# Parameter rows on GpSimd's DMA queue, a first FFN1 pass between the x transposes, a row copy on GpSimd, and a last store in three parts

## The chip, the cores and the metric

The kernel runs on one core of one Trainium2 chip. The metric is the device time of one execution in microseconds (us). The profile's span is about 1.7 us shorter than that time, because it starts and ends a little inside it. TensorE (PE), VectorE (DVE), ScalarE (ACT), GpSimd (POOL) and SyncE (SP) each have their own list of instructions in this program. DMAs are issued here from SP, ACT and, in the changed kernel, GpSimd.

## The reference

It is a gated mix of a state-space layer and a feed-forward layer, with S = 2048, D = 448, F = 1792, in bf16.

```python
g = sigmoid((x * gate_w).sum(-1, keepdims=True))
dt = exp(log_dt);  Lam = Lambda_re + 1j * Lambda_im
Lam_bar = exp(dt * Lam)
B_bar = ((Lam_bar - 1) / Lam)[:, None] * (B_re + 1j * B_im)
h[t] = Lam_bar * h[t-1] + x[t] @ B_bar.T                  # 2048 steps
a = 2 * (h @ (C_re + 1j * C_im).T).real + x * Dskip
b = silu(x @ w1) @ w2
out = g * a + (1 - g) * b
```

## The kernel before

The kernel handles even and odd rows of x apart. Each thunk goes into the list of one engine, and a tracker adds the semaphore waits. The parts that matter lie in the first 17 us. The loads of the head, in order of issue on their queues:

```python
ld_w("sp", 0)                                     # W1 rows 0..127, first 768 columns, 192 KB
for i, (eng, v) in enumerate((("sp", A_log_dt), ("sp", A_Lambda_re),
                              ("act", A_Lambda_im), ("act", A_Dskip))):
    ld(eng, R[i:i + 1, 0:D], row(v), ...)         # four rows of 0.9 KB
ld_w("act", 1)                                    # W1 rows 128..255, 192 KB
ld_w("sp", 2)
ld("act", W1E[0:64, 3, :], B_w1[384:448, :], "W1Ea")      # W1's last 64 rows ...
ld("act", W1E[64:128, 3, :], B_w1[384:448, :], "W1Ez")    # ... and a second copy
ld("sp", W1E[:, 0:3, FA:], ..., "W1Ed")           # all other columns, 768 KB
# then BB (two of 336 KB) on ACT, transposes of x on SP, and LT (transposes of BB) later
```

TensorE begins with seven matmuls on zeros, to warm up, then 16 transposes of x, then the first FFN1 pass. This pass fills six PSUM banks, with one block of W1 rows (j) after the other:

```python
warm(NWARM)
...                                # 16 transposes of x into banks 4..7, copied to XT by VectorE
def ffn1_first():
    for j in range(4):
        for fb, bank in enumerate(banks):          # banks 0..5
            pe.matmul(ps[:, bank, :], W1E[p, j, fb*128:(fb+1)*128], XT[p, j, 0:512], ...)
            if j == 1 and fb == 2: yield           # here: the parameter transpose, mm_cols
```

`mm_cols` turns the four parameter rows R into columns. VectorE copies them to PV, ACT makes exponentials and sines of them, and only after these does ACT evacuate banks 0 to 5 (silu into AT). The main FFN1 stream (the "whole" matmuls of three row blocks and the "half-row" matmuls of W1's last 64 rows, two at a time, from the two copies) takes banks in turn: 6 and 7, then 0 and 1 again. The last of the eight output tiles is stored in two parts:

```python
parts = ((slice(0, D), ["_00"]), (slice(D, 2 * D), ["_10", "_11"])) if kt == NKT - 1 else ...
```

## Time and profile before

| kernel before | us |
|---|---|
| time, median of 3 runs | 153.32 (152.78 to 153.47) |
| span of the profiled run | 152.1 |
| TensorE takes up W1's first row block | 6.24 |
| parameter transpose | 8.53 |
| main FFN1 stream starts | 13.91 |
| last VectorE instruction ends; to the span's end | 149.89; 2.2 |

The lines of the page, the chain, TensorE and the SP queue are shown in the prediction. Two more matter for what follows. First the ACT queue in the timeline (start in us from the span's start, duration of the issues, queue, what):

```profile
1.74 0.54 ACTq L208 DMA_DIRECT2D R<-in_A_Lambda_im_dram  x1
2.31 0.24 ACTq L208 DMA_DIRECT2D R<-in_A_Dskip_dram  x1
2.58 1.59 ACTq L208 DMA_DIRECT2D W1E<-in_B_w_dram  x3
```

The two small rows go first. ACT's block of W1 is issued at 2.58, which is 0.85 us after SP issued the first block (1.73). Second, the matmuls of the first pass in the view of the tile W1E (count, ns minimum/median/maximum, first and last start in us, forms):

```profile
L330 PE MATMUL ps<-XT,W1E x24: 376/379/390, 6.2 to 11.8; 128*128 128x512 bf16 x18, 64*128 64x512 bf16 x6
```

All 24 have nearly the same duration. The 0.379 us is that of one matmul from end to end; they follow each other at 0.216 us. This is the fast pace. The seven matmuls on zeros, from 1.26 us on, followed each other at about 0.427; the fast pace began among the x transposes, at 4.4 us.

### The profile page before, as it was taken

How to read it: one execution, taken by the hardware profiler on the slowest of the kernel's cores; microseconds unless marked ns; L12 is line 12 of the kernel's file. 1: busy time of each engine (PE TensorE's matmuls, PEld its weight loads, DVE VectorE, ACT ScalarE, POOL GpSimd, SP SyncE). 2: the span in 40 equal slices, each digit the busy share in tenths (PEclk: the TensorE clock that was granted, in tenths of full speed). 3: DMA queues.
4: the chain of work that ended last, by engine and by line, in shares of the span. 5: the costliest groups of instructions: out<-in, count | busy, mean ns of one | idle time of the engine just before them, and what ended most of it. 6: DMA issues, size and time to landing. Idle time of an engine off the chain costs nothing.

```text
span 152.1 us, 2020 instructions
## 1 busy us (share of the span) xinstructions
PE 146.1 (96%) x756; PEld 69.2 (46%) x756; DVE 121.1 (80%) x234; ACT 64.1 (42%) x111; POOL 5.4 (4%) x15
## 2 busy tenths in 40 slices
PE   6797999999999999999999999999999999999993
PEld 2432434344444455433555443555555555555552
DVE  1648989999999999999999999999980017876333
ACT  0358559999978513174731294513133110000000
POOL 7000220000000000000000000000000000000000
DMA  4999999989999100485280000000000001111221
GB/s 150 240 259 233 267 287 157 224 169 168 288 318 321 49 0 0 90 151 104 51 245 6 0 0 4 2 0 0 0 0 4 0 0 60 60 60 60 92 94 60
DMA packets 26401, 16.25 MB, mean 107 GB/s; under 512 B 17940, under 2 KB 25112, under 8 KB 26392
## 3 DMA queue, kind: packets, MB, share of 16 engines
q1 hardware_dynamic: 23668, 12.46, 33.7%
q10 hardware_dynamic: 2724, 3.67, 9.6%
q8 instruction: 6, 0.10, 0.3%
q14 instruction: 3, 0.02, 0.1%
HBM read 9.93 MB, written 1.84 MB: 77 GB/s over the span
## 4 chain that ended last, share of the span: by engine, by line
PE 89%; DMA 7%; SPq 1%; DVE 0%; issue 0%
PE ps L634 28%; PE ps L298 22%; PE ps L750 14%; PE ps L650 14%; DMA W1E<-in_B_w_dram 7%; PE ps L754 4%; PE ps L313 4%; PE ps L665 4%; SPq L208 1%; SPq L237 1%; DVE OT L761 0%; PE ps L667 0%
## 5 line engine op out<-in xcount | busy, mean ns | idle before, releaser
L634 PE MATMUL ps<-W,AT 128*128 128x448 bf16 x224 | 43.0, 352 | 0.0
L340 ACT ACTIVATE AT<-ps 128x512 bf16<-128x512 f32 x56 | 29.2, 620 | 13.0 <-PE ps L313 12.5
L634 PEld LDWEIGHTS ps<-W,AT 128*128 128x128 bf16 x224 | 21.8, 98 | 20.6 <-issue 0.2
L639 ACT ACTIVATE LT<-ps,GT 128x448 bf16<-128x448 f32 x16 | 10.1, 634 | 31.3 <-PE ps L634 27.6
L650 PE MATMUL ps<-XT,LT 128*128 128x512 bf16 x98 | 21.3, 379 | 0.0
L298 PE MATMUL ps<-XT,W1O 128*128 128x512 bf16 x84 | 19.1, 379 | 0.0
L761 DVE SCALAR_TENSOR_TENSOR OT<-ps,GT,LT 128x448 bf16<-128x448 f32 x8 | 5.5, 684 | 14.8 <-PE ps L754 14.7
L686 DVE TENSOR_TENSOR_SCAN G<-P,Q 128x1024 f32<-128x1024 f32 x7 | 15.7, 2278 | 0.0
L298 PE MATMUL ps<-XT,W1E 128*128 128x512 bf16 x66 | 14.9, 380 | 0.1
L650 PEld LDWEIGHTS ps<-XT,LT 128*128 128x128 bf16 x98 | 9.6, 98 | 11.5
L298 PEld LDWEIGHTS ps<-XT,W1O 128*128 128x128 bf16 x84 | 7.9, 98 | 10.6 <-issue 1.7
L750 PE MATMUL ps<-CO,HS 128*128 128x448 bf16 (+1 forms) x63 | 11.9, 332 | 0.0
L750 PE MATMUL ps<-CE,HS 128*128 128x448 bf16 x56 | 11.9, 352 | 0.0
L298 PEld LDWEIGHTS ps<-XT,W1E 128*128 128x128 bf16 x66 | 6.1, 98 | 8.7 <-issue 1.3
L654 ACT ACTIVATE HS<-ps 128x512 bf16<-128x512 f32 x14 | 8.5, 633 | 3.2 <-PE ps L650 2.7
L761 DVE SCALAR_TENSOR_TENSOR OT<-ps,GT,W1E 128x448 bf16<-128x448 f32 (+1 forms) x9 | 5.7, 632 | 4.7 <-PE ps L750 4.7
L601 DVE SCALAR_TENSOR_TENSOR JK<-W1O,GWB 128x448 bf16<-128x448 bf16 x16 | 8.8, 618 | 0.0
L683 DVE TENSOR_TENSOR Q<-G,SIN 128x1024 bf16<-128x1024 f32 x7 | 8.5, 1219 | 0.0
L683 DVE TENSOR_TENSOR Q<-G,COS 128x1024 bf16<-128x1024 f32 x7 | 8.5, 1209 | 0.0
L750 PEld LDWEIGHTS ps<-CO,HS 128*128 128x128 bf16 x63 | 6.1, 98 | 4.7
L750 PEld LDWEIGHTS ps<-CE,HS 128*128 128x128 bf16 x56 | 5.5, 98 | 5.1
L754 PE MATMUL ps<-KT,XT 128*128 128x448 bf16 x32 | 7.4, 352 | 0.0
(84 smaller groups left out, 145.3 us busy)
## 6 DMA issues: line engine op xcount, KB each, us to landing
W1O<-in_A_x_dram ACTq DMA_DIRECT2D x1, 1792.0 KB, 14.4
W<-in_B_w_dram SPq DMA_DIRECT2D x1, 1568.0 KB, 8.1
out_dram<-OT SPq DMA_DIRECT2D x7, 224.0 KB, 2.0
W1O<-in_B_w_dram SPq DMA_DIRECT2D x1, 1344.0 KB, 8.7
W1E<-in_A_x_dram SPq DMA_DIRECT2D x1, 896.0 KB, 6.1
W1E<-in_B_w_dram SPq DMA_DIRECT2D x1, 768.0 KB, 10.6
W1E<-in_B_w_dram ACTq DMA_DIRECT2D x2, 224.0 KB, 8.1
W1O<-in_B_w_dram SPq DMA_DIRECT2D x2, 224.0 KB, 5.0
```

What stands on the lines that cost most here:

```text
L298: ins = pe.matmul(ps[:, bank, :], W[:, w0 + j, fb * 128:(fb + 1) * 128], XT[:, x0 + j, hs], start=(j == 0 and not rest_first), stop=(j == ...
L340: T.op("act", lambda e: e.activation(a[:, fb, :], ps[:, bank, :], AF.Silu), reads=[f"ps{bank}"], writes=[f"AT{c % 2}_{fb}"])
L601: T.op("dve", lambda e, t=t: e.scalar_tensor_tensor(JK[:, t % 2, :], XN[:, t * D:(t + 1) * D], 1.0, GWB[:, :], ALU.mult, ALU.mult, accum_o ...
L634: ins = pe.matmul(ps[:, bank, 0:D], a[:, fb, q * 128:(q + 1) * 128], W2[:, fb, :], start=(fb == 0), stop=(fb == NFB - 1))
L639: T.op("act", lambda e: e.activation(bs(tile), ps[:, bank, 0:D], AF.Copy, scale=GT[:, 2, tile:tile + 1]), reads=[f"ps{bank}", "GT2"], writ ...
L650: ins = pe.matmul(ps[:, bank, :], LT[:, m, j, :], XT[:, j, h * 512:(h + 1) * 512], start=(j == 0), stop=(j == 6))
L654: T.op("act", lambda e: e.activation(HS[:, m, 8 + h * 512:8 + (h + 1) * 512], ps[:, bank, :], AF.Copy), reads=[f"ps{bank}", f"F{pt}"], wri ...
L683: T.op("dve", lambda e: e.tensor_tensor(o, a, b, op), reads=reads, writes=writes)
L686: T.op("dve", lambda e: e.tensor_tensor_scan(G[:, c, :], rb, Q1[:, c, :], 0.0, ALU.mult, ALU.add), reads=[f"Q1{c}", "rr"], writes=[f"G{c}"])
L750: ins = pe.matmul(ps[:, b, c], HS[:, m, o0:o0 + 128], C[:, m, c], start=(m == 0), stop=(odd == 1 and m == 6))
L754: ins = pe.matmul(ps[:, b, c], XT[:, j, t0:t0 + 128], KT[:, j, c], start=False, stop=(j == 3))
L761: T.op("dve", lambda e, b=b, c=c: e.scalar_tensor_tensor(o[:, odd * D:(odd + 1) * D][:, c], ps[:, b, c], GT[:, 1, tile:tile + 1], (BG[:, k ...
```

## The change

The four parts aim at the head and the tail. (1) The parameter rows go on GpSimd's queue, so that SP and ACT are free for W1 sooner. (2) TensorE transposes only half of the x tiles, runs the j = 0 part of the first pass, and transposes the rest. (3) The second copy of W1's last 64 rows is no longer loaded but copied by GpSimd. (4) The last store is in three parts.

```diff
         ld_w("sp", 0)
-        for i, (eng, v) in enumerate((("sp", A_log_dt), ("sp", A_Lambda_re), ("act", A_Lambda_im), ("act", A_Dskip))):
-            ld(eng, R[i:i + 1, 0:D], row(v), f"R{i}", gR if i < 2 else gR2)
         ld_w("act", 1)
         ld_w("sp", 2)
         ld("act", W1E[0:64, 3, :], B_w1[384:448, :], "W1Ea")
-        ld("act", W1E[64:128, 3, :], B_w1[384:448, :], "W1Ez")
 ...
+        for i, v in enumerate((A_log_dt, A_Lambda_re, A_Lambda_im, A_Dskip)):
+            ld("pool", R[i:i + 1, 0:D], row(v), f"R{i}", gR)
 ...
+        for i, c in enumerate((slice(FA, FA + 512), slice(FA + 512, F_FF), slice(0, FA))):
+            T.op("pool", lambda e, c=c: e.tensor_copy(W1E[64:128, 3, c], W1E[0:64, 3, c]), reads=["W1Ea"],
+                 writes=[f"W1Ez{i}"])
 ...
-                    if j == 1 and fb == 2:
+                    if (j, fb) in ((0, NFA - 1), (1, 2)):
                         yield
 ...
+        xpose(0)
+        xpose(1)
         first = ffn1_first()
         next(first)
-        T.op("pe", mm_cols, reads=["R0", "R1", "R2", "R3", "Rd", "ID"], writes=["ps7"])
+        xpose(2)
+        xpose(3)
+        rd()
+        next(first)
+        T.op("pe", mm_cols, reads=["R0", "R1", "R2", "R3", "Rd", "ID"], writes=["ps6"])
 ...
-            parts = ((slice(0, D), ["_00"]), (slice(D, 2 * D), ["_10", "_11"])) if kt == NKT - 1 else \
+            parts = ((slice(0, D), ["_00"]), (slice(D, D + 224), ["_10"]), (slice(D + 224, 2 * D), ["_11"])) \
```

Smaller companions, cut here: the warm-up operand is 128 columns wide and read four times over, the parameter transpose uses bank 6, and the XR half swaps of VectorE stand behind the first exponentials.

More of the change, by code (lines that the diff above doesn't have):

```diff
@@ L221, in swap_xr @@
                  writes=[f"XR{h}b"])
-        T.op("dve", lambda e: e.memset(Q1[:, 0, 0:512], 0.0), writes=["Q10"])
+        T.op("dve", lambda e: e.memset(Q1[:, 0, 0:128], 0.0), writes=["Q10"])
         T.op("dve", lambda e: e.memset(SG[0:64, 0:1], -1.0), writes=["SGa"])
@@ L226, in gated_mix @@
         T.op("dve", lambda e: e.memset(HP[:, :], HALF_PI), writes=["HP"])
-        gR, gR2, gB = T.group(), T.group(), T.group()
+        gR, gB = T.group(), T.group()
         def row(v):
@@ L305, in rest @@
             def rest():
-                wk = ["W1Oa", "W1Oz"] if odd else ["W1Ea", "W1Ez"]
                 for i in range(0, len(fbs), 2):
+                    z = [fb * 128 - FA for fb in fbs[i:i + 2]]
+                    wk = ["W1Oa", "W1Oz"] if odd else ["W1Ea"] + sorted(
+                        {"W1Ez2" if v < 0 else "W1Ez0" if v < 512 else "W1Ez1" for v in z})
                     def mm(pe, i=i):
@@ L357, in mm_cols @@
             for pt in range(4):
-                ins = pe.matmul(ps[:, 7, pt * 8:pt * 8 + 4], R[0:4, pt * 128:(pt + 1) * 128],
+                ins = pe.matmul(ps[:, 6, pt * 8:pt * 8 + 4], R[0:4, pt * 128:(pt + 1) * 128],
                                 ID[0:4, 0:4], start=True, stop=True)
@@ L361, in warm @@
         def warm(n):
+            z = Q1[:, 0, 0:128].rearrange("p (a b) -> p a b", a=1).to_broadcast([128, 4, 128])
             def mm(pe):
@@ L364, in mm @@
                 for _ in range(n):
-                    ins = pe.matmul(ps[:, 7, :], Q1[:, 0, 0:128], Q1[:, 0, 0:512], start=True, stop=True)
+                    ins = pe.matmul(ps[:, 7, :], Q1[:, 0, 0:128], z, start=True, stop=True)
                 return ins
@@ L369, in gated_mix, with xpose @@
         warm(NWARM)
-        xp = [ps[:, 4 + j, 0:256].bitcast(BF16) for j in range(4)]
-        for i in range(2):
-            for j in range(4):
-                def mm(pe, j=j, i=i):
-                    ins = None
-                    for k in (2 * i, 2 * i + 1):
-                        ins = pe.transpose(xp[j][:, k * 128:(k + 1) * 128], XH[:, k, j * 128:(j + 1) * 128], ID[:, :])
-                    return ins
-                T.op("pe", mm, reads=COK[2 * i:2 * i + 2] + ["ID"], writes=[f"ps{4 + j}"])
-        for j in range(4):
-            T.op("dve", lambda e, j=j: e.tensor_copy(XT[:, j, 0:512], xp[j]), reads=[f"ps{4 + j}"], writes=[f"XTe0{j}"])
-        rd()
-        T.op("dve", lambda e: e.tensor_copy(XR[64:128, 0:512], xp[3][0:64, :]), reads=["ps7"], writes=["XR0a"])
-        T.op("dve", lambda e: e.tensor_copy(XR[0:64, 0:512], xp[3][64:128, :]), reads=["ps7"], writes=["XR0b"])
+        xb = [4, 5, 6, 7]
+        xp = [ps[:, b, 0:256].bitcast(BF16) for b in xb]
+        def xpose(j):
+            for k in range(4):
+                T.op("pe", lambda pe, k=k: pe.transpose(
+                    xp[j][:, k * 128:(k + 1) * 128], XH[:, k, j * 128:(j + 1) * 128], ID[:, :]),
+                    reads=COK[k:k + 1] + ["ID"], writes=[f"ps{4 + j}"])
+            T.op("dve", lambda e: e.tensor_copy(XT[:, j, 0:512], xp[j]), reads=[f"ps{4 + j}"], writes=[f"XTe0{j}"])
+        xpose(0)
+        xpose(1)
         first = ffn1_first()
         next(first)
-        T.op("pe", mm_cols, reads=["R0", "R1", "R2", "R3", "Rd", "ID"], writes=["ps7"])
+        xpose(2)
[3 more added lines that the diff above has]
+        T.op("pe", mm_cols, reads=["R0", "R1", "R2", "R3", "Rd", "ID"], writes=["ps6"])
+        T.op("dve", lambda e: e.tensor_copy(
+            PV[:, :, :], ps[:, 6, 0:32].rearrange("p (t c) -> p t c", c=8)[:, :, 0:4]),
+            reads=["ps6"], writes=["PV"])
         first = next(first)
-        T.op("dve", lambda e: e.tensor_copy(
-            PV[:, :, :], ps[:, 7, 0:32].rearrange("p (t c) -> p t c", c=8)[:, :, 0:4]),
-            reads=["ps7"], writes=["PV"])
         names = {}
@@ L422, in gated_mix @@
         T.op("act", lambda e: e.activation(JK[:, 0, 0:1], HP[:, :], AF.Silu), reads=["HP"], writes=["JK0"])
+        T.op("dve", lambda e: e.tensor_copy(XR[64:128, 0:512], xp[3][0:64, :]), reads=["ps7"], writes=["XR0a"])
+        T.op("dve", lambda e: e.tensor_copy(XR[0:64, 0:512], xp[3][64:128, :]), reads=["ps7"], writes=["XR0b"])
         ptt("ph", col("dt"), LIM, ALU.mult, ["dt", "PV"])
@@ L588, in load_xo @@
             T.dma("sp", lambda e: e.dma_start(XO, x2.rearrange("(k p) c -> p k c", p=128)[:, :, D:]),
-                  writes=["XO", "W1Ez", "W1Ea", "W1Ed", "W1Ej0", "W1Ej1", "W1Ej2"])
+                  writes=["XO", "W1Ez0", "W1Ez1", "W1Ez2", "W1Ea", "W1Ed", "W1Ej0", "W1Ej1", "W1Ej2"])
         def skip(kt):
@@ L769, in store @@
             o = OT[kt % 3]
-            parts = ((slice(0, D), ["_00"]), (slice(D, 2 * D), ["_10", "_11"])) if kt == NKT - 1 else \
-                ((slice(0, 2 * D), ["_00", "_10"]),)
+            parts = ((slice(0, D), ["_00"]), (slice(D, D + 224), ["_10"]), (slice(D + 224, 2 * D), ["_11"])) \
+                if kt == NKT - 1 else ((slice(0, 2 * D), ["_00", "_10"]),)
             for i, (c, ks) in enumerate(parts):
-                outs.append(T.dma("sp" if i or len(parts) == 1 else "act", lambda e, c=c: e.dma_start(out2[kt * 128:(kt + 1) * 128, c], o[:, c]),
+                outs.append(T.dma("act" if i == 1 else "sp", lambda e, c=c: e.dma_start(out2[kt * 128:(kt + 1) * 128, c], o[:, c]),
                                   reads=[f"OT{kt % 3}{k}" for k in ks], writes=[f"out{kt}{i}"]))
```

## The prediction

> **What bounds the kernel now.** I read the page first (busy shares, slices, chain), then the chain in order of time, then TensorE and the queues in the first 35 us, last the final 8 us. From the page: busy shares of the engines, DMA busy tenths in 40 slices of 3.8 us, the chain's shares.
>
> ```profile
> PE 146.1 (96%) x756; PEld 69.2 (46%) x756; DVE 121.1 (80%) x234; ACT 64.1 (42%) x111; POOL 5.4 (4%) x15
> DMA  4999999989999100485280000000000001111221
> PE 89%; DMA 7%; SPq 1%; DVE 0%; issue 0%
> ```
>
> TensorE is the bound; the only large piece of the chain that is not TensorE is a DMA into W1E, 7%. In order of time (start us, us, what):
>
> ```profile
> 3.24 10.62 DMA W1E<-in_B_w_dram
> 13.86 0.05 issue
> 13.91 5.35 PE ps L298 x24
> ...
> 148.06 1.36 PE ps L750 x14
> 149.42 0.02 issue
> 149.44 0.45 DVE OT L761
> ```
>
> From 13.91 to 149.42 the chain has nothing but TensorE pieces that join without a gap: 135.5 us of fixed work, which this change does not shorten. The list of waits for TensorE has no wait of over 0.2 us after 14 us except the "issue" ones of the weight loads, which lie beside matmuls. So the change can act only on the 13.9 us before and the 2.7 us after. TensorE in the head (start, duration, idle before):
>
> ```profile
> 4.21 1.14 PE L376 MATMUL ps<-ID,CO 128*128 128x128 bf16 x16
> 6.24 2.35 PE L330 MATMUL ps<-XT,W1E 128*128 128x512 bf16 x9 [0.88 <-DMA W1E<-in_B_w_dram]
> 8.53 0.25 PE L358 MATMUL ps<-ID,R 4*128 4x4 bf16 x4
> 8.71 3.51 PE L330 MATMUL ps<-XT,W1E 128*128 128x512 bf16 x15
> 13.24 0.39 PE L313 MATMUL ps<-XT,W1E 64*128 64x512 bf16 x1 [1.02 <-DMA W1E<-in_B_w_dram]
> ```
>
> All 16 x transposes end at 5.35, TensorE waits for W1's first rows until 6.24, makes the first FFN1 pass (24 matmuls) until 12.2, waits for the second copy of W1's last 64 rows until 13.24 and for the big column block of W1 until 13.91. The queues say who makes those two late (issue time, duration; and from the view of DMA issues between 3.6 and 4.1 us, KB and us to landing, the second copy):
>
> ```profile
> 2.19 0.33 SPq L208 DMA_DIRECT2D R<-in_A_log_dt_dram  x1
> 2.57 0.22 SPq L208 DMA_DIRECT2D R<-in_A_Lambda_re_dram  x1
> 2.84 0.83 SPq L208 DMA_DIRECT2D W1E<-in_B_w_dram  x2
> ...
> W1E<-in_B_w_dram ACTq DMA_DIRECT2D x1, 224.0 KB, 9.6
> ```
>
> The second copy is issued at about 3.6 and lands at 13.2. The column block is issued at 3.24, after two R rows. And there is a second limit close behind the first, the transposed BB tile that the next stage (L650) reads:
>
> ```profile
> 27.30 9.27 SPq L211 DMA_TRANSPOSE LT<-BB  x7
> ...
> LT<-BB SPq DMA_TRANSPOSE x1, 3.1
> ...
> 30.74 7.50 PE L650 MATMUL ps<-XT,LT 128*128 128x512 bf16 x34
> ```
>
> 27.30 + 3.1 = 30.4: the first LT tile lands some 0.3 us before TensorE starts on it. If TensorE comes a microsecond earlier and LT does not, the gain is lost there. LT waits for its place on the SP queue, behind all the loads of the head.
>
> **What the Trainium skill says.** "DMA: Bandwidth & Descriptors", section "Issuing engines are not separate DMA queues": transfers from SP, ACT and GpSimd run on the same 16 DMA engines, so another issuer saves only issue time. The trace agrees that the engines are the limit: they are at 9 tenths or more in nearly every slice from the second to the 13th, whichever queue issued. The same page, "Specifications" and "Anatomy of one DMA": a GpSimd DMA has its first byte at about 1 us (0.6 from SP or ACT) and a fixed cost of about 2 us. No GpSimd DMA is in this trace, so nothing here confirms it. "SBUF — State Buffer", "Who interferes with whom": GpSimd and certain VectorE modes exclude each other on a port pair, also while GpSimd writes descriptors. The x copies read PSUM and, by that section, should not do so; the two GpSimd copies in this trace (1.14 and 0.66 us for the same 64x512) vary, which may be that.
>
> **The change part by part.**
>
> *Second copy of W1's last rows on GpSimd.* Removes 224 KB of DMA. Between 8.5 and 12.3 us the DMA engines moved 223 GB/s (view by windows), so 0.229 MB / 223 GB/s = 1.0 us of all DMA engines. It lies ahead of BB on the ACT queue and beside the column block on SP's. Since BB's loads move up into the gap, the block gets only part of it: I take 0.5 us. But everything later in the saturated head, LT included, gets nearly all, 0.9. It adds three GpSimd copies. From the two above: 0.7 to 1.1 us for each 512 columns. The rows themselves landed at 9.6 (6.6 us after an issue near 3.0), say 9.1 now; the piece that the first stage needs is there at 10 to 10.5, before TensorE asks for it at about 12.3. Hidden.
>
> *R rows on GpSimd's queue.* Frees 0.33 + 0.22 us plus gaps, about 0.65 us (2.19 to 2.84), ahead of the column block on SP, and 0.54 + 0.24 us on ACT ahead of the W1 rows. The block is issued 0.65 us earlier; with engines already saturated from 2 us on I count 0.4 of it. R itself is issued on GpSimd from about 1.4 us; estimate from the skill's figures: four at up to 1 us each, then 2 us, so landing at 6 to 7.5 us. It is needed by the column transpose of the parameters, on TensorE at about 8. Just enough.
>
> *First pass between the x transposes.* In the kernel before, the transposes are over at 5.35 and W1's first rows come at 6.2, so they were already hidden. Now half of them (8, 1.14/2 = 0.57 us) come after the first 6 matmuls. W1's second row block comes some 0.7 us earlier than the 7.77 at which TensorE took it up, which pays for it. First pass: 6.2 + 24 x 0.216 us + 0.57 + 0.25 = 12.2, as before, or a few tenths later if it stands waiting for R. (0.216: 0.81 us of three overlapping matmuls less 0.38 of one, halved.)
>
> *Sum of the head.* Block at 13.86 - 0.4 - 0.5 = 12.95; the 8 half-row matmuls before it (about 0.5 us) fit between 12.3 and 12.9. Main stream starts at 13.0 instead of 13.91: **-0.9 us**. LT comes 0.9 earlier and has 0.3 to spare: it does not take the gain back. The smaller memset starts the warm-up matmuls 0.2 us earlier; they end before the x tiles have landed, so nothing.
>
> *Last store in three.* The last part is issued at the same moment (149.9), but with 56 KB instead of 112 KB. It landed 1.7 us after the issue, as did the other 112 KB store, while 224 KB took 1.9 to 2.0: so about 0.2 us per 112 KB, and half as much saves **0.1 us**.
>
> Sum -1.0. I take back 0.2 for the chance that R is late. 153.32 - 0.8 = 152.5.
>
> **The rivals.**
> 1. *R is late and becomes the new wait.* Four GpSimd DMAs in a row are unmeasured here. TensorE, VectorE (the XR copies now stand behind PV) and ACT (its exponentials stand before the evacuations of the first pass) all queue behind R in order. For: three in-order engines depend on it, and TensorE reaches it at about 8 us. Against: a slack of about 1 us after the first pass takes some of it. R at 9 us makes the gain zero; R at 12 costs 1.5 to 2 us, 155.
> 2. *The transfer is hidden anyway.* BB and the later transposes refill the DMA engines, the block comes only 0.3 us earlier, or LT only 0.3: 152.9 to 153.2. For: engines saturated, round about equal sharing between queues. Against: 224 KB really vanish.
> 3. *More is won than I count.* If the block comes at 12, TensorE's own first pass (12.2 plus 0.5) becomes the bound: at most 1.2 us plus 0.2 from the store, 151.9; a faster first pass by a tighter clock ramp 151.5.
>
> **Range and chances.** Prediction 152.5. Rival 3 sets the low end, 151.5; rival 2 and a mild rival 1 the high end, 153.6. 2% is 3.07 us: faster would need the stream to start at 10.9 us, sooner than the first pass can end; slower needs R at over 13 us. Chances 0.02, 0.94, 0.04.
>
> **What would show it.** Right: the chain's DMA piece into W1E ends near 12.9 and the stream starts at 13.0; no stretch of idle TensorE before the L650 stage; the first LT landing near 29.5; R landed before 8; GpSimd's W1E copies over before 12 (all three by 13.5); last landing 0.1 us nearer to the last VectorE instruction. Wrong: an idle TensorE of over 0.5 us at the parameter transpose with R as releaser (rival 1); a DMA landing of W1E still after 13.5, or a wait of TensorE on LT of over 0.3 us (rival 2); W1E's landing before 12.3 (rival 3). The prediction would be badly wrong if a GpSimd DMA has a start-up cost of several microseconds, or if VectorE holds GpSimd up.

## The result and the profile after

The changed kernel took 157.47 us (median of 4 runs: 156.56, 157.66, 157.29, and 160.08 in the slow state). The kernel before, beside it, took 153.26. The ratio of the fast runs is 1.026 (95%: 1.0205 to 1.0315), so it is **slower**. Here and below, a ratio is the mean time of one kernel's fast runs over that of the other's of the same rounds, so not quite the ratio of the medians. A later set of four runs on another chip gave 156.51 and 1.0171 (e15 below), so the loss is 1.7 to 2.6%. The profiled run of after is a fast one (156.56, span 154.8); that of before took 153.78.

The page of after, busy shares and the chain's shares:

```profile
PE 148.3 (96%) x748; PEld 70.5 (46%) x756; DVE 121.3 (78%) x234; ACT 63.6 (41%) x111; POOL 9.0 (6%) x22
PE 93%; DMA 4%; issue 1%; SPq 1%; DVE 0%
```

The chain's DMA share fell from 7% to 4%, yet the kernel is slower. TensorE is busy for 2.2 us more, although no matmul was added. The chain in order of time (start us, us, what):

```profile
1.72 5.65 DMA W1E<-in_B_w_dram
...
7.42 2.74 PE ps L334 x6
...
17.04 5.13 PE ps L300 x23
...
152.35 0.45 DVE OT L771
```

The chain is no longer held by the large column block but by W1's first block, issued at 1.72 and landed some 5.65 us later. Then TensorE runs to the end. The stream starts at 17.04 instead of 13.91 (+3.13), and its last VectorE instruction starts at 152.35 instead of 149.44 (+2.91). So **the whole loss arises before the stream**, as the stream's own length (135.3 against 135.5 us) did not grow. TensorE in the head:

```profile
4.01 1.15 PE L381 MATMUL ps<-ID,CO 128*128 128x128 bf16 x8
7.42 2.74 PE L334 MATMUL ps<-XT,W1E 128*128 128x512 bf16 x6 [2.25 <-DMA W1E<-in_B_w_dram]
9.95 1.06 PE L381 MATMUL ps<-ID,CO 128*128 128x128 bf16 x8
10.81 1.49 PE L334 MATMUL ps<-XT,W1E 128*128 128x512 bf16 x3
12.23 0.26 PE L362 MATMUL ps<-ID,R 4*128 4x4 bf16 x4
```

Before, TensorE idled 0.88 us and then did nine matmuls in 2.35 us. Now it idles 2.25 us. Six matmuls take 2.74 us by the chain until the transposes follow, and three more take 1.28, which is 4.02 for nine, or 0.45 each with their tails, where 0.216 had been the pace. The view of the tile W1E shows the same matmuls as slow ones:

```profile
L334 PE MATMUL ps<-XT,W1E x24: 376/403/634, 7.4 to 16.0; 128*128 128x512 bf16 x18, 64*128 64x512 bf16 x6
```

The maximum went from 390 to 634 ns. Since when TensorE is slow is told by the x transposes ahead of the pass (view of their line, before and then after):

```profile
L376 PE MATMUL ps<-ID,CO x16: 219/219/304, 4.2 to 5.1; 128*128 128x128 bf16 x16
L381 PE MATMUL ps<-ID,CO x16: 286/314/314, 4.0 to 10.7; 128*128 128x128 bf16 x16
```

In after they are slow too, before the wait and behind it. So TensorE did not lose the fast pace in this run; it had not reached it, and did so at 13.3 us only. The packed trace agrees: its first record of a full granted clock begins at 13.32 us. (The views count the time ahead of the first record as full, so the mean clock of 1.000 hides this.)

The parameter transpose comes at 12.23 instead of 8.53, which is +3.70 and divides into three terms:

| term | us |
|---|---|
| W1's first block: 7.42 instead of 6.24 | +1.18 |
| nine matmuls: 4.02 instead of 2.35 | +1.67 |
| eight transposes that now stand between them (chain) | +0.85 |
| sum | +3.70 |

Of this, 3.13 reach the stream: before, TensorE had still some idle time behind the transpose, waiting for the second copy of W1's last rows.

The issues of after, in the timeline (the last one is the load of x for the gates):

```profile
1.45 0.66 POOL L208 DMA_DIRECT2D R<-in_A_log_dt_dram  x1
1.72 1.38 SPq L208 DMA_DIRECT2D W1E<-in_B_w_dram  x3
1.74 1.01 ACTq L208 DMA_DIRECT2D W1E<-in_B_w_dram  x2
...
9.49 2.16 POOL L273 COPY W1E<-W1E 64x512 bf16<-64x512 bf16 x3 [3.32 <-DMA W1E<-in_B_w_dram]
...
16.79 0.45 ACTq L208 DMA_DIRECT2D W1O<-in_A_x_dram  x1
```

ACT's block of W1 is now issued at 1.74, beside SP's first block, not 0.85 us behind it. GpSimd's copies end at 11.65. In the view of DMA issues (KB each, us to landing), the last row and the column block:

```profile
R<-in_A_Dskip_dram POOLq DMA_DIRECT2D x1, 0.9 KB, 6.9
W1E<-in_B_w_dram SPq DMA_DIRECT2D x1, 768.0 KB, 9.5
```

The last row was issued at 3.06 and landed at 9.9. The block was issued at 2.67 and landed at 12.2, earlier than the predicted 12.95, but no one waits for it any more. The tail is shorter: from the end of the last VectorE instruction to the span's end it is 2.01 us instead of 2.16.

### The profile page after: what moved, and what is told of

Read it like the earlier page. It is cut to its first block, busy times and chain, and to the rows that moved or that the text cites. A ratio compares the mean times of both kernels' runs of the same rounds, so it can differ in the third digit from the quotient of the medians.

```text
span 154.8 us, 2015 instructions
## 1 busy us (share of the span) xinstructions
PE 148.3 (96%) x748; PEld 70.5 (46%) x756; DVE 121.3 (78%) x234; ACT 63.6 (41%) x111; POOL 9.0 (6%) x22
## 4 chain that ended last, share of the span: by engine, by line
PE 93%; DMA 4%; issue 1%; SPq 1%; DVE 0%
PE ps L644 27%; PE ps L300 21%; PE ps L760 14%; PE ps L660 14%; PE ps L334 5%; PE ps L317 4%; PE ps L764 4%; DMA W1E<-in_B_w_dram 4%; PE ps L675 3%; PE ps L381 1%; SPq L237 1%; DVE OT L771 0%; PE ps L677 0%; PE ps L362 0%
## 5 line engine op out<-in xcount | busy, mean ns | idle before, releaser
L344 ACT ACTIVATE AT<-ps 128x512 bf16<-128x512 f32 x56 | 28.7, 624 | 12.4 <-PE ps L317 12.4
L300 PE MATMUL ps<-XT,W1O 128*128 128x512 bf16 x80 | 18.3, 379 | 0.4 <-issue 0.3
L334 PE MATMUL ps<-XT,W1E 128*128 128x512 bf16 (+1 forms) x24 | 8.2, 495 | 2.3 <-DMA W1E<-in_B_w_dram 2.3
L384 DVE COPY XT<-ps 128x512 bf16<-128x512 bf16 x4 | 1.7, 425 | 8.5 <-PE ps L381 8.5
```

The lines of the kernel that those rows point to most:

```text
L300: ins = pe.matmul(ps[:, bank, :], W[:, w0 + j, fb * 128:(fb + 1) * 128], XT[:, x0 + j, hs], start=(j == 0 and not rest_first), stop=(j == ...
L334: T.op("pe", lambda pe, fb=fb, bank=bank, j=j, p=p: pe.matmul(ps[:, bank, :], W1E[p, j, fb * 128:(fb + 1) * 128], XT[p, j, 0:512], start=( ...
L344: T.op("act", lambda e: e.activation(a[:, fb, :], ps[:, bank, :], AF.Silu), reads=[f"ps{bank}"], writes=[f"AT{c % 2}_{fb}"])
```

## The experiments

**The theory** after reading these traces: the two rows on ACT had held back ACT's block of W1, so that SP's first block, which TensorE needs first, had the DMA engines nearly to itself. Without them the two blocks share the engines, the first one lands 1.2 us later, and the array, idle for longer after a shorter burst (only half of the transposes), falls to its slow pace. (This last step was put wrongly: the array had not been fast yet. "The pace" below has what the traces show.) **Rivals**: that GpSimd's DMAs themselves disturb the loads, or that the rows come too late (the prediction's first rival); that the new order costs the time by itself; that the ramp differs by chance from run to run and the change has no part in it. Fifteen kernels were run, all with correct results. Every profiled run counts as fast; its mean granted clock is 0.989 in e3 and e15 and 0.999 or 1.0 in all others, with the time ahead of the first record counted as full. Ratios are against the kernel before.

| run | edit | median us (runs) | ratio, fast runs [95%] |
|---|---|---|---|
| after | the change | 157.47 (4) | 1.026 [1.0205, 1.0315] |
| e15 | the change again | 156.51 (4) | 1.0171 [1.0083, 1.0258] |
| e5 | before + part 1 | 155.88 (4) | 1.0147 [1.0109, 1.0184] |
| e7 | before + part 2 | 155.00 (20) | 1.0032 [1.0005, 1.0058] |
| e6 | before + part 3 | 153.45 (20) | 1.0012 [0.9992, 1.0032] |
| e2 | after without part 1 | 154.28 (20) | 1.0061 [1.0039, 1.0082] |
| e3 | after, all transposes first | 155.40 (4) | 1.0147 [1.0095, 1.0198] |
| e1 | after + fill of the idle stretch | 155.17 (4) | 1.0107 [1.0058, 1.0157] |
| e4 | after + 4 dummy rows on SP and ACT | 155.10 (16) | 1.0098 [1.0067, 1.0129] |
| e13 | after + 2 dummy rows on SP | 155.93 (4) | 1.0127 [1.0044, 1.021] |
| e14 | after + 2 dummy rows on ACT | 155.91 (4) | 1.0137 [1.0068, 1.0205] |
| e9 | before, rows behind ACT's W1 block | 153.67 (20) | 1.0025 [1.0007, 1.0043] |
| e10 | e7 + fill | 153.52 (20) | 1.0031 [1.0011, 1.005] |
| e11 | e1 + earlier load of x for the gates | 155.22 (4) | 1.013 [1.0085, 1.0176] |
| e8 | before + parts 3 and 4 + other cut of the stream | 152.45 (20) | 0.9949 [0.9928, 0.9969] |
| e12 | e8 + fill | 152.81 (22) | 0.998 [0.9963, 0.9996] |

The median is of all runs of the kernel, the ratio of the fast ones alone. Part 4 was not run alone.

### Each part by itself, and all but one

**e5, part 1 alone**, on the kernel before:

```diff
-        for i, (eng, v) in enumerate((("sp", A_log_dt), ..., ("act", A_Dskip))):
-            ld(eng, R[i:i + 1, 0:D], row(v), ...)
+        for i, v in enumerate((A_log_dt, A_Lambda_re, A_Lambda_im, A_Dskip)):
+            ld("pool", R[i:i + 1, 0:D], row(v), f"R{i}", gR)
```

> The kernel before with only the parameter rows moved to GpSimd's queue. If the rows' move alone is the main cause: W1's first block lands at 7.4 us instead of 6.2, the rows at about 10, TensorE meets the parameter transpose at 9.5 and waits for the rows, stream start 15 to 16.5 us, 155 to 156.5. If it needs the split of the transposes too (theory O, by way of the clock): the long first burst keeps the fast matmul pace, loss under 1.2 us, 154.4 or less.

It is slower by 1.5%, most of the loss. TensorE in the head of this run:

```profile
7.36 3.62 PE L330 MATMUL ps<-XT,W1E 128*128 128x512 bf16 x9 [1.23 <-DMA W1E<-in_B_w_dram]
11.74 0.23 PE L358 MATMUL ps<-ID,R 4*128 4x4 bf16 x4 [0.75 <-DVE XR L383]
```

The first block is late by 1.12 us (7.36 against 6.24), the nine matmuls take 1.27 us longer (3.62 against 2.35), though all 16 transposes ran before them (slow as well: 1.91 us instead of 1.14), and TensorE waits 0.75 us for the rows, which VectorE took up at 10.52 (behind it stand the XR copies, which the transpose's bank waits for). So the late row costs 0.8 us here, in the old order. These add up to the 3.2 us by which the parameter transpose is late (11.74 against 8.53).

**e7, part 2 alone** (after with parts 1, 3 and 4 undone; the edit is part 2's of the diff above):

> The kernel before with only the reordered first pass (passes between the x transposes, smaller memset, x half swaps moved behind the first parameter product). Theory O: the first burst of TensorE work is shorter by 8 transposes, so the fast matmul pace is missed in a part of the executions: a spread of times, some at 153.3 and some 1.5 to 2 us longer, median 154 to 155. If the order is harmless: 153.0 to 153.5 with the spread of before.

The fast runs are 0.3% slower, but 9 of 20 runs lay over 1.5% above this kernel's fastest and are counted as slow, so its all-run median is 1.7 us up. The profiled run had the fast pace in the first pass (six matmuls in 1.47 us after an idle 1.70) and a stream start of 13.88, like the kernel before. No upper run was profiled, but six of the 20 runs (155.02 to 156.41) have a mean granted clock of 0.989; see "The pace".

**e6, part 3 alone** (the `W1Ez` load replaced by the three copies, as in the diff):

> The kernel before with only the second copy of W1's last 64 rows made by GpSimd. The prediction's step for this part: W1's column block and the second copy are there by 12.3 us or sooner, main stream starts at 13.0 to 13.4, time 152.6. Rival (the wait behind it): TensorE's second pair of half-row matmuls waits for ScalarE's evacuation of banks 0 and 1, as in the run with rows on SP and ACT, where that held it until 13.31: stream start 13.5 to 13.9, time within 0.3 us of before.

It is the same (1.0012). Its column block landed at 11.2 us, 2.6 earlier than before (13.86), more than I had counted, and LT's first tile at 27.9 instead of 30.4. Still the stream started at 13.53, only 0.4 us earlier. The line that stands in the way:

```profile
12.17 0.38 PE L317 MATMUL ps<-XT,W1E 64*128 64x512 bf16 x1
13.21 0.39 PE L317 MATMUL ps<-XT,W1E 64*128 64x512 bf16 x1 [0.66 <-ACT AT L344]
```

The second pair of half-row matmuls needs banks 0 and 1 again, and ACT empties them only after the exponentials and sines of the parameters. ACT, in the kernel before (both banks) and in e6 (bank 1):

```profile
11.37 1.06 ACT L340 ACTIVATE AT<-ps 128x512 bf16<-128x512 f32 x2
12.56 0.59 ACT L344 ACTIVATE AT<-ps 128x512 bf16<-128x512 f32 x1
```

In the kernel before the banks were empty at 12.43, 0.8 us ahead of the end of the DMA wait (13.24), so the wait on ACT lay hidden. In e6 they are empty at 13.15. The parameter transpose was only 0.11 us later (8.64); the rest comes from VectorE's part of the parameter chain. While the three GpSimd copies ran (9.24 to 11.43), one VectorE instruction beside each took 0.50, 0.57 and 0.66 us, and ended within 0.03 us of the copy's end; their like take 0.15 to 0.18 in the kernel before. The same stretching stands beside these copies in e2, e8, e12 and e14. So the copy that was to be hidden is itself part of the new wait. How large a part in the other runs of e6 wasn't measured.

**e2, all but part 1** (the rows back on SP and ACT, the rest as after):

> The changed kernel with the four parameter rows back on the SP and ACT queues, all else kept. Theory S (with the rows gone, ACT's second W1 block is issued beside the first one and takes half of its transfers): the first block lands at 6.2 us again instead of 7.4, TensorE idles 1 us, and the time falls to 153 to 154.5. Theory R (rows land too late through GpSimd: 9.9 us): same fall, but the first block stays at 7.4 and only the parameter transpose moves. Theory O (order of the first pass and the transposes is the loss): stays at 156.5 to 157.5.

Part 1 costs 1 to 2% on top of the other three (1.0061 here, 1.026 and 1.0171 with it). In the profile the first block is there at 5.5 and the parameter transpose is at 8.36, both even earlier than before; the next wait is ACT's again:

```profile
13.31 0.39 PE L317 MATMUL ps<-XT,W1E 64*128 64x512 bf16 x1 [1.04 <-ACT AT L344]
```

Its profiled span is 151.6, shorter than before's 152.1, while its fast runs are on average 0.6% slower. The profiled run was the fastest of its 20 (153.38, range to 156.05), and that of before was above its median (153.78). What its longer runs spend wasn't profiled and stays open; like e7, it holds the new order and has a wide spread.

### The pace

**e1, fill.** Five more matmuls on zeros between the first transposes and the pass keep the array busy while it waits:

```diff
         xpose(1)
+        warm(5)
         first = ffn1_first()
```

> The changed kernel with five more dummy matmuls (128x512) on TensorE after the first eight x transposes, so that it does not stand idle for 2.25 us while W1's first rows are on their way. In the changed kernel the first 14 matmuls of the first FFN1 pass came 0.43 us apart, against 0.216 in the kernel before. Theory C (a slow array clock after the idle stretch is most of the loss): the pass runs at 0.216 us a matmul from its start, the main stream starts near 14.3 us instead of 17.0, time about 154.5. Theory S (late first rows of W1 are the loss) and theory R (late parameter rows): the pass still starts at 7.4, stream and time within 0.5 us of the changed kernel, 157.

```profile
7.90 1.47 PE L334 MATMUL ps<-XT,W1E 128*128 128x512 bf16 x6 [1.27 <-DMA W1E<-in_B_w_dram]
...
33.03 4.27 PE L661 MATMUL ps<-XT,LT 128*128 128x512 bf16 x19 [0.76 <-DMA LT<-BB]
```

The six matmuls take 1.47 instead of 2.74 us although the block came later (7.90) and TensorE was idle for 1.27 us behind the fill, and the stream starts at 15.28, 1.76 us earlier than in after. But 0.76 of that is given back at LT, and the span is only 0.6 us shorter. (The profiled run of e1 was its slowest, 155.96, and that of after its fastest, 156.56; the medians differ by 2.3, by 1.3 from e15.) The pace is a true term of the loss, and a second limit stands behind it: LT.

**e3, all transposes ahead of the pass**, with the other parts as in after:

```diff
         xpose(1)
-        first = ffn1_first()
-        next(first)
         xpose(2)
         xpose(3)
         rd()
+        first = ffn1_first()
+        next(first)
         next(first)
```

> The changed kernel with all 16 x transposes ahead of the first FFN1 pass again, all else kept (rows on GpSimd). Theory O (half the transposes in the middle of the pass, and a shorter first burst of TensorE work, cost the clock and 1 us of transposes): TensorE's first burst is long enough, the pass runs fast from its start, time 153 to 154.5. Theory S: the pass still starts at 7.4 us after 1.7 us of idling, the fast clock may or may not hold; 155 to 157.

The median is 155.40, 1.1 us better than e15 and 2.1 better than after (the intervals overlap with e15's), so the new order is at most a part of the loss. The first block still comes at 7.64 after an idle 1.56 us, nine matmuls take 3.68 us, and the stream starts at 15.82. Here the fast pace was indeed lost: the granted clock is recorded as full from 4.03 us, as half from 7.44 to 10.86, and as full again.

**e10, part 2 alone with a fill** of four matmuls on zeros in the idle stretch (`warm(4)` after `xpose(1)`):

> The reordered first pass alone, which gave times from 152.8 to 157.8 in two clusters, with four dummy matmuls in the idle stretch after the first eight transposes. Theory C (the clusters are executions with a fast and with a slow matmul pace in the first pass): the upper cluster goes away, all runs 152.8 to 153.9, median 153.4. If the spread has another cause it stays, median near 155.

No run of 20 counts as slow (e7: 9 of 20). The fast runs of the two are equal (1.0031 and 1.0032), so the fast ones show only that the spread is narrower (152.71 to 154.53). But the six runs at a mean granted clock of 0.989 are gone as well: none of e10's 20 is below 0.999. A single stretch of 3.41 us at half clock makes this 0.989 (half of 3.41 is 1.1% of 154 us; e15's trace, below, shows one). So for these runs of e7 the cause is the lost pace, and the fill prevents it. The other upper runs, at 0.999 and 1.0, stay open. It also means that the slow runs left out of e7's ratio are in part the kernel's own cost.

**What tips the pace.** The 17 traces, read together, show it. The records of the granted clock change in steps of 3.41 us (143.36 us at full clock in after is 42 of them), and the steps begin at a different place in each run. All runs begin slow and turn fast at the end of the first step in which TensorE hardly idles; where there are records, the matmuls change pace where the clock does. (Idle time in a step: its length less PE's busy time, from the view by windows.)

| runs | idle in the step, us | pace behind it |
|---|---|---|
| 13 runs, fast from 4.0 to 6.5 us on | up to 0.44 | becomes fast |
| e14 (2.46 to 5.88), e5 (3.63 to 7.04), after (3.08 to 6.49, then to 9.91) | 0.76, 0.91, 1.33 and 0.93 | stays slow |
| e7, e4 (from 4.4) | 1.70, 1.74 | stays fast |
| e3 (4.03 to 7.44), e15 (4.85 to 8.26) | 2.06, 2.37 | becomes slow |

(e13's trace has no clock records; its pace turned fast at about 10.1 us, behind a step with about 0.78 us idle, so the limit lies near there.) So a wait of over 2 us for the first block costs the pace wherever most of it falls into one step: it spoils the step that would make TensorE fast (after), or it undoes it (e15). That is worked out from the traces; what was tried as a change is the fill, in e1, e10 and e11.

### Who delays W1's first block

**e4, four dummy rows.** After, with four more loads of the same rows into an unused tile, at the places on SP and ACT where the rows had been:

```diff
         ld_w("sp", 0)
+        for i, (eng, v) in enumerate((("sp", A_log_dt), ("sp", A_Lambda_re), ("act", A_Lambda_im), ("act", A_Dskip))):
+            ld(eng, RD[i:i + 1, 0:D], row(v), f"RD{i}", gD)
         ld_w("act", 1)
```

> The changed kernel with the rows used still coming through GpSimd, but four dummy loads of the same rows into an unused tile where the kernel before issued them on SP and ACT. It tells S from R. Theory S: the issue of W1's second block is held back as before, the first block lands at 6.2 us, time as in the run with rows on SP and ACT, within 0.5 us. Theory R, or the GpSimd descriptors themselves slowing W1: the first block stays near 7.4, time stays at 156.5 or more.

Loads that nobody reads seem to make the kernel faster (155.10 against 157.47 and 156.51; the interval overlaps that of e15 though not that of the first after), with the first block at 6.67 instead of 7.42 and the fast pace. Both are less than expected (6.2 us, and within 0.5 us of e2's 154.28). GpSimd's DMAs are the same as in after, so they alone don't explain the delay. e13 and e14 split this by queue, on one chip together with e15 (after again):

**e13, dummies on SP alone**, the first two of the four:

> The changed kernel with two dummy row loads on SP alone, between W1's first and third block. With the loads on both queues the first block landed at 6.6 us and the time was 155.1; without any at 7.3 to 7.9 and 157.5. If the spacing on SP is what gives the first block its start: it lands at 6.3 to 6.8 here, time near 155. If it is the spacing on ACT: 7.3 to 7.8, time 156.5 to 157.5.

**e14, dummies on ACT alone**, the last two:

> The changed kernel with two dummy row loads on ACT alone, ahead of W1's second block. If the hold on ACT's second block is what counts: first block at 6.3 to 6.8 us, time near 155. If SP's spacing counts, or both are needed: 7.0 to 7.8, time 156 to 157.5. The run with the rows one place later on ACT gave 6.8, between the two, so I expect ACT to bring about half.

**e15, after again**, unchanged:

> The changed kernel itself once more, beside these two: 156.5 to 158, first block of W1 at 7.2 to 7.8 us, slow matmul pace until 10 us or later, stream start 16 to 17.2. If the profiled execution of the first time was an odd one, first block or pace differ.

The first block, in us from issue to landing: e15 5.6, e13 5.6, e14 4.2. So it is ACT's block, held back by two tiny DMAs, that lets SP's first block through, and SP's own rows have no part in it. One profile each would be thin, but all 17 agree: the first block took 3.5 to 4.9 us in the nine that issue ACT's block at 2.6 us, with GpSimd's rows (e4, e14) or without, 5.6 to 6.1 in the seven with ACT's block at 1.7 and the rows on GpSimd, and 5.1 in e9. But no gain in time is shown for e14 (155.91 against 156.51, with intervals that overlap). TensorE in its head:

```profile
6.01 2.74 PE L338 MATMUL ps<-XT,W1E 128*128 128x512 bf16 x6 [0.90 <-DMA W1E<-in_B_w_dram]
8.55 0.97 PE L385 MATMUL ps<-ID,CO 128*128 128x128 bf16 x8
10.12 0.82 PE L338 MATMUL ps<-XT,W1E 128*128 128x512 bf16 x3 [0.61 <-DMA W1E<-in_B_w_dram]
```

The first block came 1.4 us earlier, but the pace was slow until 9.29 us, and the second block, now the later one (7.5 us from issue to landing, 6.0 in e15), made TensorE wait 0.61 us. The stream started at 16.04, in e13 at 16.36 and in e15 at 15.97. In e15 four matmuls were fast and the next slow: the granted clock is recorded as full from 4.85, half from 8.26 to 11.68, and full again.

**e9, rows behind ACT's W1 block**, on the kernel before:

```diff
         ld_w("sp", 0)
+        ld_w("act", 1)
         for i, (eng, v) in enumerate((("sp", A_log_dt), ...)):
             ld(eng, R[i:i + 1, 0:D], row(v), ...)
-        ld_w("act", 1)
```

> The kernel before, the rows still on SP and ACT, but issued one place later: on ACT behind W1's second block instead of ahead of it. No GpSimd DMA at all. Theory S (the two small loads held the second block back by 0.8 us and gave the first one a start): the first block lands at 7.0 to 7.6 us instead of 6.2, TensorE idles about 1.7 us after the transposes and the time is 154 to 155.5. Rival (GpSimd's own descriptors slow W1 down): the first block stays at 6.2 to 6.5 and the time at 153.3.

The time is the same (1.0025), not the 154 to 155.5 that the theory had forecast: a first block that is 0.6 us late costs next to nothing in the old order, whose profiled run kept the fast pace and had the DMA wait behind it. The first block took 5.1 us, between the 4.5 of before and the 5.6 of after (e15; 5.7 in the first), with no DMA on GpSimd at all. So the order on ACT makes about half of the delay here. What makes the rest is open, as the figure is from one profile: GpSimd's rows, the run, or ACT's next loads, which are issued from 3.06 us here and from about 2.2 in after.

### LT, and a version that is faster

**e11: e1, with the 1.8 MB load of x for the gates** issued on ACT right behind BB and not after the first evacuations:

```diff
         ld("act", BB[:, 1:6:2, D:], ..., "Bim", gB)
+        ld("act", W1O..., x2.rearrange("(k p) c -> p k c", p=128), "XN")
 ...
-        load_xn()                   # the same load, behind the first evacuations
```

> The changed kernel with the five dummy matmuls, and the 1.8 MB load of x for the gates issued on ACT right behind BB instead of after the first evacuations. In the run with the fill alone TensorE stood at LT for 0.8 us, because that load was issued at 14.8 us instead of 12.7 and shared the DMA engines with the x transposes until 31.3. Theory (late evacuations delay that load, it delays the transposes, they delay LT): LT's first tile lands at 28 to 30.5 us, no wait of TensorE on LT, time 154 or less against 155.2. Rival: the early load only slows W1 and the x transposes; no gain.

LT's first tile landed at 26.7 us and TensorE didn't wait for it any more; the profiled span was 153.0 against e1's 154.2 (its own fastest run against e1's slowest). The median didn't improve (155.22 against 155.17), so a gain isn't shown; inconclusive.

**e8: parts 3 and 4 on the kernel before, and another cut of the stream.** Since e6 showed that banks 0 and 1 are the wait, the first chunk takes only the two banks that are free:

```diff
-            for f in range(f0, NFB, 4):
-                for fb, bank in ffn1_mm(c, list(range(f, min(f + 4, NFB))), rest_first):
+            cuts = (6, 8, 12, 14) if f0 else (0, 4, 8, 12, 14)
+            for f, f1 in zip(cuts, cuts[1:]):
+                for fb, bank in ffn1_mm(c, list(range(f, f1)), rest_first):
```

> A version made from what the runs show: the kernel before (rows on SP and ACT, all x transposes first), with the second copy by GpSimd and the last store in three, and the blocks of FFN1's first chunk cut 2, 4, 2 instead of 4, 4, so that TensorE has 6 full matmuls to do before it needs banks 0 and 1 from ScalarE. If ScalarE's evacuation is the next wait, the stream starts at about 12.2 us and the time is 151.6 to 152.2; if LT's landing takes it back, a stall of up to 1 us near 29 us and 152.5; if the copy by GpSimd itself is late, no better than before.

It beats both kernels, the one before by 0.5%: 152.45, ratio 0.9949, and a span of 150.6. The stream starts at 12.39, straight behind the first pair of half-row matmuls, and LT's first tile is there at 27.7. TensorE:

```profile
12.08 0.38 PE L317 MATMUL ps<-XT,W1E 64*128 64x512 bf16 x1
12.39 1.90 PE L300 MATMUL ps<-XT,W1E 128*128 128x512 bf16 x8
```

Against e6 (13.53) the cut is what turned an early block into an early stream, though in e8's profile ACT had also emptied banks 0 and 1 by 12.50 already.

**e12: e8 with three matmuls on zeros** (`warm(3, 3)`, into bank 3) between the transposes and the pass:

> The version that beat both kernels (152.45), with three dummy matmuls between the x transposes and the first pass against the idle 1.1 us there. If a slow pace in part of the executions is what spreads its times (151.8 to 153.3), the spread narrows and the median is 152.0 to 152.3; if not, the same 152.4.

It has a narrower spread (152.24 to 153.14 in 22 runs) but no gain on e8; that it is slower isn't shown (other rounds, on another chip, and the intervals touch). In the profiled run the 16 transposes were still slow and took 1.91 us (1.14 in the kernel before), so the zeros began at 5.92 only and the pass at 6.64 instead of 6.21. A fill is only free where it ends before the data come.

## Why the prediction was right or wrong

It predicted 152.5 us with a range of 151.5 to 153.6 and gave slower by over 2% a chance of 4%; the kernel took 157.47. The direction was wrong. By its own steps:

1. **"W1's second row block comes some 0.7 us earlier ... which pays for it"**: this step failed first. It took the first block's 6.2 us as fixed and counted an earlier issue on ACT as pure gain. The first block came at 7.42, for ACT's block was issued beside it. The dummies on ACT alone (e14) took 1.4 us off its landing and those on SP alone (e13) none. The prediction named the rule (the queues share the engines) and used it for the big block only. This term is +1.18 us.
2. **"6.2 + 24 x 0.216 us"**: the pace was taken as a constant. Nine matmuls took 4.02 instead of 2.35 us (+1.67). e1 shows that this is the array's pace and not a wait: with a fill six of them took 1.47 instead of 2.74. A clock ramp was named only as an upside, in the third rival, although the kernel before showed both paces: 0.427 us for the first matmuls, 0.216 from 4.4 us on. In after the longer wait kept TensorE at the first until 13.3 us.
3. **"they were already hidden. Now half of them (8, 1.14/2 = 0.57 us)"**: the transposes between the matmuls were put in, as 0.57, and measured 0.85 in the slow pace and 0.45 in the fast one (e7 and e1). A right step; the 0.40 between is the pace again.
4. **"the 8 half-row matmuls before it (about 0.5 us) fit between 12.3 and 12.9"**, and with it the -0.9: wrong, shown by e6. Even with the block at 11.2, TensorE stood until 13.21 for ACT's evacuations behind the parameter chain. The list of waits of the kernel before showed only the DMA, which came last (13.24); that on ACT, which would have ended at 12.43, was not in it. And the GpSimd copies, called hidden, moved it to 13.15 by stretching VectorE's part of the chain. The prediction had named that GpSimd and VectorE exclude each other, but asked it only of the x copies and of GpSimd's own speed. e8 shows the gain once the stream doesn't need these banks.
5. **Rows "landing at 6 to 7.5 us"**: they landed at 9.9. In after this had no own cost, as TensorE was later still; in e1 and e13 it cost 0.27 and 0.54 us, in e5 0.75. So rival 1 holds for part 1 alone, but "slower needs R at over 13 us" fell: slower came with R at 9.9, for the two terms above.
6. **"LT comes 0.9 earlier"**: right wherever the stream was not late (27.9 in e6, 27.7 in e8, against 30.4), wrong in after, where it landed at 33.4: the big load of x for the gates waits on ACT behind the evacuations and was issued at 16.79 instead of 12.65, to share the engines with the transposes ahead of LT. That this load is what delays LT is supported by e11 (26.7 us), not isolated.
7. **Right**: the column block earlier (12.2, predicted 12.95), GpSimd's copies over before 12 (11.65), TensorE's 135.5 us from the stream's start on (135.3), and the store (2.16 to 2.01, so 0.15 for the predicted 0.1). All four are true, and none of them helps while the stream starts late.

Of the 2.9 us, then, part 1 made the most (e5 and e2), through the order of issue and the pace; part 2 put eight transposes behind the wait and shortened the burst ahead of it. What is open: the other half of the first block's delay in e9, and what e2, and e7 in its upper runs at full mean clock, lose in the runs that weren't profiled.

## What to carry to other kernels

Ahead of full DMA engines, ask of each load not only when it is issued but which load it will then run beside: a tiny DMA ahead of a large one can be what lets the first block through. When a wait is taken away, look for the one that ended before it, which the list of waits doesn't show, follow the engine it hangs on (here ACT's evacuations behind the parameter chain), and ask what the change itself does to that engine's inputs. Where TensorE waits in its first microseconds, price the wait twice, once as idle time and once as the slower matmuls that can follow it, and read the pace from the spacing of the matmuls: the mean clock of after was given as 1.000, with the slow pace until 13.3 us.

## What the Trainium skill lacked or had wrong

- "TensorE: Matmul & The Clock Gate", Part 1, "What's actually happening": the clock is at half by default and at full after a busy window of about 3.4 us, and the window runs free of the kernel's start. The runs agree (0.427 us a matmul of 512 columns when slow, 0.216 when fast; clock records in steps of 3.41 us that begin at another place in each run). What it lacks is how much idle time a window bears: here up to 0.44 us still won the full clock and 0.9 did not, and 1.74 kept it. For the fall back it gives an idle window of about 3.4 us; here steps with 2.06 and 2.37 us of idle time in 3.41 were enough (e3, e15). It puts the ramp at under 1% of a typical span and warns that it varies; in after it was 1.67 us in nine matmuls, 1.1% of 154.8.
- "DMA: Bandwidth & Descriptors", "Issuing engines are not separate DMA queues": it says that issuing from several engines saves only the time of the issue. The runs add that the order among the queues decides which transfer lands first: two loads of 0.9 KB ahead of ACT's block brought SP's block from 5.6 to 4.2 us (e15, e14).
- The same page, "Specifications" and "Anatomy of one DMA": about 1 us to the first byte and 2 us fixed for GpSimd's DMAs. Beside full engines, four of 0.9 KB took 3.3 to 6.9 us to land (after), and their issues 0.66 and three times 0.49 us of GpSimd.
- Neither of these two pages says that evacuations which stand behind a scalar chain on ACT can be the next wait of TensorE; it was 0.66 us in e6 and 1.04 in e2.
